# Raw w_in four pieces ahead, combine one expert earlier, last w2 in thirds of columns, every second w_out block decoded with ScalarE

## The chip, the cores and the metric

The kernel runs on one core of one Trainium2 chip. The metric is device microseconds of one execution; the time given is the median of three. One profiled execution stands beside it.

## The reference

The input goes through attention, then a soft mixture of eight experts, then a gated layer. Attention makes x, 1792 tokens of 768 columns; it is the same in both kernels and takes the first 309 us. Then:

```
# mixture: 8 experts, 4 slots each
logits = x @ phi                                # 1792 x 32
d = softmax of logits over the tokens           # dispatch
slot_input = d.T @ x                            # 32 x 768
for e in range(8):
    h = maximum(slot_input[e] @ w1[e], 0)       # 4 x 1024
    slot_out[e] = h @ w2[e]                     # 4 x 768
c = softmax of logits over the slots            # combine
y = c @ slot_out                                # 1792 x 768
# gated layer
h = y @ w_in                                    # 1792 x 2048
g = h * 1 / (1 + exp(-1.702 * h))
out = g @ w_out                                 # 1792 x 768
```

w_in and w_out arrive as 64-bit floats and are made into 32-bit ones on the chip. That is the decode spoken of below.

## The kernel before

**The expert loop** (from 309 us). For each expert e TensorE multiplies the slot inputs with w1[e] (h, L1071), VectorE makes hs = max(h, 0) scaled (L1082), TensorE transposes hs (t, L1092), VectorE copies it to hTz (L1097, L1098), and for the first six experts TensorE multiplies with w2[e] into so_ps (L1102). Fillers (L1061) keep TensorE busy in experts 5 to 7. The weights come in pieces through SP's queue (w1 L114, w2 L123) into buffers that TensorE has read last; reload (L131) asks for the next weights as soon as a half is used. The w2 of the last two experts (L117) comes in twelve pieces of 128 columns, all 1024 rows of one expert in each, and is multiplied after the loop, because slot_out is wanted there column by column.

**Decode.** w_in is cut into 24 pieces of 128 x 512, raw 512 KB each. win_load (L988) asks for one on ScalarE's queue; the tiles wst are a ring of six. win_turn is called after each of the 14 steps of an expert; from turn 29 on, every 2.2 turns, it takes one piece j: first the load of j+5, then the four steps of decode64 (L136): ScalarE scales the high words into dst (L143), VectorE shifts (L145), puts the sign in (L147) and the low bits in (L151). hs and the decode steps stand in VectorE's queue in program order.

**Combine.** combine (L1017) takes the softmax over the slots on VectorE and ScalarE at the start of expert 2, and combine_turn (L1029) makes its transposed parts, four of them, during that expert.

**After the loop** the work is put in order by a planner with a table of operations, each with an engine, a cost and a due time: last_mm (L1173) for the last w2, its copy pc (L1188), transpose pt (L1191) and sum pa (L1195), then u (L1209): slot_out @ w_in, which needs all of w_in. u0 (L1360) copies u for the first tokens. Then each token's hidden columns f come out of TensorE (L1258), ScalarE makes gg (L1266) and rounds it to gh (L1275), VectorE makes the rest gl (L1280), and TensorE multiplies with w_out (y, L1316 for the first tokens, L1299 for the rest). w_out is decoded during the first tokens, in 16 blocks of 128 rows: raw load (L1139), decode64's steps (abs on ScalarE, wd 0, 1, 2 on VectorE), whi rounds it on ScalarE (L1158) and wlo makes the rest on VectorE (L1162).

## Time and profile before

| what | us |
|---|---|
| median of 3 runs | 712.28 (710.15 to 713.52) |
| profiled execution | 712.17 |
| its span | 710.40 |
| TensorE busy | 633.2, 89% of the span |
| VectorE busy | 389.7 |
| ScalarE busy | 346.9 |

The share of busy time is a mean over stages. The table of windows gives, for a stretch, the busy time of each engine, the granted clock of TensorE as a share of full speed, the share of time that the DMA engines were busy, and the rate. A timeline row gives start, duration, engine, line, the operation with its output and inputs, and in brackets how long the engine was idle before it and what ended that.

### The profile page before, as it was taken

What the parts mean: (1) busy time and instruction counts of PE and PEld (TensorE: products, weight loads), DVE (VectorE), ACT (ScalarE), POOL (GpSimd) and SP (SyncE); (2) the same over time, 40 slices, a digit from 0 to 9 for tenths busy, and PEclk for the clock granted to TensorE, in tenths of its full rate; (3) what the DMA queues carried; (4) which work ended last, traced back from release to release, by engine and by line L of the source; (5) the groups of instructions that cost most, each with busy time, mean ns of one, the idle gap of its engine ahead of it and who ended that gap; (6) DMA issues with size and microseconds to landing.
All of it is one profiled execution on the core that took longest, in us unless ns stands there. A gap on an engine that the chain in (4) does not pass through costs nothing.

```text
span 710.4 us, 11049 instructions
## 1 busy us (share of the span) xinstructions
PE 633.2 (89%) x4091; PEld 414.3 (58%) x4091; DVE 389.7 (55%) x672; ACT 346.9 (49%) x730; POOL 193.3 (27%) x233
## 2 busy tenths in 40 slices
PE   1899999999999999986452699889999999999997
PEld 1333434443344334543221235789999999999997
DVE  5997678787887885325554712799911211211211
ACT  3766977777798764522211220766612332422432
POOL 4765988877665623200000010000000000000000
PEclk9999999999999999999666899899999999999999
DMA  9399899798989898669999982556010100100101
GB/s 225 74 178 224 195 204 232 160 199 185 228 208 192 183 253 222 240 229 398 404 403 410 330 209 90 198 172 208 22 46 1 66 2 0 67 1 1 66 2 45
DMA packets 152310, 120.30 MB, mean 169 GB/s; under 512 B 102048, under 2 KB 133024, under 8 KB 152256
## 3 DMA queue, kind: packets, MB, share of 16 engines
q1 hardware_dynamic: 148448, 106.85, 56.2%
q10 hardware_dynamic: 3744, 12.65, 4.7%
q8 instruction: 32, 0.52, 0.3%
q14 instruction: 22, 0.18, 0.1%
q0 software_dynamic: 64, 0.10, 0.1%
HBM read 92.18 MB, written 5.51 MB: 138 GB/s over the span
## 4 chain that ended last, share of the span: by engine, by line
PE 65%; DVE 14%; DMA 12%; issue 3%; ACT 3%; POOL 2%; SPq 1%; ACTq 0%; DVEq 0%; POOLq 0%
PE y L1299 26%; PE sc L517 7%; PE pv L536 6%; DMA wr<-in_moe_w_dram 6%; PE mx L498 4%; PE so_ps L1102 3%; PE pv L531 2%; PE h L1071 2%; DVE wr L502 2%; DMA wr<-wr 2%; DMA wt<-in_moe_w_dram 2%; PE y L1316 1%; DVE wr L439 1%; DVE wf L147 1%; PE f L1258 1%
## 5 line engine op out<-in xcount | busy, mean ns | idle before, releaser
L1280 DVE TENSOR_TENSOR gl<-gg,gh 128x384 fp32r<-128x384 f32 (+1 forms) x80 | 42.2, 530 | 149.0 <-ACT gh L1275 147.8
L502 DVE TENSOR_REDUCE wr<-mx 128x2 f16<-128x896 f32 x92 | 89.7, 975 | 27.8 <-PE mx L498 27.3
L1266 ACT ACTIVATE gg<-f 128x384 f32<-128x384 f32 (+1 forms) x78 | 36.5, 470 | 124.7 <-PE f L1258 121.3
L1299 PE MATMUL y<-wo,gh 128*128 128x384 f32 x352 | 75.4, 335 | 0.0
L524 POOL TENSOR_TENSOR es<-es,e 128x448 f32<-128x448 f32 x47 | 55.2, 1184 | 29.5 <-PE pv L536 10.1
L1299 PEld LDWEIGHTS y<-wo,gh 128*128 128x128 f32 x352 | 62.1, 188 | 0.0
L521 ACT ACTIVATE e<-sc,esc 128x448 f32<-128x448 f32 x96 | 56.7, 638 | 11.1 <-PE sc L517 10.3
L1299 PE MATMUL y<-wh,gl 128*128 128x384 f32 x176 | 46.8, 337 | 0.0
L1299 PE MATMUL y<-wh,gh 128*128 128x384 f32 x176 | 46.7, 336 | 0.0
L1299 PE MATMUL y<-wl,gh 128*128 128x384 f32 x176 | 46.7, 336 | 0.0
L1299 PE MATMUL y<-wo,gl 128*128 128x384 f32 x176 | 44.9, 335 | 0.0
L1275 ACT ACTIVATE gh<-gg 128x384 fp32r<-128x384 f32 (+1 forms) x78 | 39.3, 504 | 6.6 <-PE y L1299 4.2
L388 ACT ACTIVATE wr<-wr 128x512 f32<-128x512 f32 (+1 forms) x48 | 28.7, 607 | 27.1 <-DMA wr<-in_k_dram 13.5
L143 ACT ACTIVATE wi<-wst 128x512 f32<-128x512 f32 x24 | 15.7, 668 | 53.6 <-DMA wr<-in_moe_w_dram 22.4
L521 ACT ACTIVATE es<-sc,esc 128x448 f32<-128x448 f32 x54 | 33.0, 636 | 18.1 <-PE sc L517 18.1
L439 POOL TENSOR_TENSOR wr<-wr 128x512 f32<-128x512 f32 (+1 forms) x33 | 33.7, 1044 | 4.8 <-DVE wr L424 4.3
L517 PEld LDWEIGHTS <-wr 128*128 128x128 f16 (+1 forms) x224 | 18.6, 103 | 24.5 <-issue 17.4
L498 PE MATMUL mx<-wr 64*128 64x448 f16 (+1 forms) x120 | 31.0, 366 | 1.4 <-DVE wr L502 1.3
L1299 PEld LDWEIGHTS y<-wl,gh 128*128 128x128 f32 x176 | 32.0, 188 | 0.0
L1299 PEld LDWEIGHTS y<-wh,gl 128*128 128x128 f32 x176 | 32.0, 188 | 0.0
L1299 PEld LDWEIGHTS y<-wo,gl 128*128 128x128 f32 x176 | 31.8, 188 | 0.0
L1299 PEld LDWEIGHTS y<-wh,gh 128*128 128x128 f32 x176 | 31.6, 188 | 0.0
(268 smaller groups left out, 1341.1 us busy)
## 6 DMA issues: line engine op xcount, KB each, us to landing
wr<-in_moe_w_dram SPq DMA_DIRECT2D x30, 512.0 KB, 9.2
wt<-in_moe_w_dram SPq DMA_DIRECT2D x24, 512.0 KB, 8.0
wst<-in_moe_w_in_dram ACTq DMA_DIRECT2D x24, 512.0 KB, 6.8
wr<-in_moe_w_out_dram SPq DMA_DIRECT2D x15, 768.0 KB, 4.7
wr<-in_moe_w_dram SPq DMA_DIRECT2D x20, 384.0 KB, 5.5
wt<-in_moe_w_dram SPq DMA_DIRECT2D x20, 384.0 KB, 7.7
out_dram<-o SPq DMA_DIRECT2D x13, 384.0 KB, 2.3
wr<-in_q_dram SPq DMA_DIRECT2D x12, 384.0 KB, 4.8
```

The source lines that it names most:

```text
L388: nc.scalar.activation(out=sqt[p][:, 8:] if i else sqt[p][:, :8], in_=rows(p, i), func=AF.Square, scale=D ** -0.5)
L439: eng.tensor_tensor(out=n, in0=n, in1=r.to_broadcast([P, m, D]), op=ALU.mult)
L498: nc.tensor.matmul(out, q_cols(QAT[p], h, c)[:D], k_cols(KBT[p], h)[:D], start=True, stop=True)
L502: nc.vector.tensor_reduce(out=of(qb_t, p)[:, at[0]:at[-1] + 1:max(1, at[-1] - at[0]), D:D + 1], in_=MX.pop((p, g))[:, :len(at), :S], axis= ...
L517: nc.tensor.matmul(out, k_cols(a, n, c), q_cols(b, n), start=first, stop=not first)
L521: nc.scalar.activation(out=E[p, h, c], in_=SC.pop((p, h, c)), func=AF.Exp, scale=esc)
L524: on(f"e{h}{c}", p)[0].tensor_tensor(out=E[p, h, 0], in0=E[p, h, 0], in1=E[p, h, c], op=ALU.add)
L536: nc.tensor.matmul(PV[p][h * D:(h + 1) * D, :], t[:, 6 * n + 3 * h + c], E[p, h, c], start=(c == 0), stop=False)
L1266: nc.scalar.activation(out=ggt[w][:, :w[1]], in_=src[:, :w[1]], func=AF.Silu, scale=1.702)
L1275: nc.scalar.activation(out=gh[:, :w[1]], in_=ggt[w][:, :w[1]], func=AF.Copy)
L1280: nc.vector.tensor_tensor(out=G[w][1][:, :n], in0=ggt[w][:, :n], in1=G[w][0][:, :n].bitcast(F32), op=ALU.subtract)
L1299: nc.tensor.matmul(Y[t, u][:, :384], a[:, ts], b[f][:, u * 384:(u + 1) * 384], start=(f == 0 and i == 0), stop=(f == KF - 1 and i == 2),)
```

## The change

Five things are changed.

- The raw pieces of w_in: the first five loads are issued on SP's queue, where the loads during the loop stay on ScalarE's. The load at turn j is for piece j+4, no longer j+5, in the same ring of six.
- Their decode: the form called low has a second ScalarE step on the low words, in place, and two VectorE steps in place of three.
- combine is called in expert 0, after the third of its six products, and its turns in expert 1.
- The last w2 comes in thirds of 256 columns, 512 rows of one expert in a piece; the order is third, expert, half of the rows. Products of two neighbouring blocks of columns use the same pieces, and wait for both halves.
- w_out: odd blocks f use the form low. whi now follows the last decode step, and wlo follows whi. The planner's costs and due times for these are adapted.

```diff
@@ -113,10 +113,10 @@
                 r = hh * 384 + n * 128
                 nc.sync.dma_start(out=t[:, n * F1:(n + 1) * F1], in_=w1[e, r:r + 128, :])
             elif e == EL:
-                c, ee = divmod(3 * hh + n, 2)
+                c, ee, fh = (3 * hh + n) // 4, (3 * hh + n) // 2 % 2, (3 * hh + n) % 2
                 nc.sync.dma_start(
-                    out=t[:, n * F1:(n + 1) * F1].rearrange("p (f c) -> p f c", c=128),
-                    in_=w2[EL + ee, :, c * 128:(c + 1) * 128].rearrange("(f p) c -> p f c", p=128),
+                    out=t[:, n * F1:(n + 1) * F1].rearrange("p (f c) -> p f c", c=256),
+                    in_=w2[EL + ee, fh * 512:fh * 512 + 512, c * 256:(c + 1) * 256].rearrange("(f p) c -> p f c", p=128),
                 )
             else:
                 r = hh * 512 + n * 128
@@ -133,24 +133,32 @@
         if is_kept[key] is not None and nstream[0] < len(stream) - (0 if is_kept[key] else NW):
             load_all(wt[key], is_kept[key])
 
-    def decode64(dst, src, i):
+    def decode64(dst, src, low):
 
 
 
         pair = src.rearrange("p (a two) -> p a two", two=2)
         hi, lo, bits = pair[:, :, 1], pair[:, :, 0], dst.bitcast(U32)
-        if i == 0:
-            nc.scalar.activation(out=dst, in_=hi.bitcast(F32), func=AF.Copy, scale=2.0 ** -112)
-        elif i == 1:
-            nc.vector.tensor_scalar(out=bits, in0=bits, scalar1=3, scalar2=None, op0=ALU.logical_shift_left)
-        elif i == 2:
-            nc.vector.scalar_tensor_tensor(
-                out=bits, in0=hi, scalar=0x80000000, in1=bits, op0=ALU.bitwise_and, op1=ALU.bitwise_or
-            )
+        join = lambda out, a, n, b, op: nc.vector.scalar_tensor_tensor(
+            out=out, in0=a, scalar=n, in1=b, op0=op, op1=ALU.bitwise_or
+        )
+        steps = [lambda: nc.scalar.activation(out=dst, in_=hi.bitcast(F32), func=AF.Copy, scale=2.0 ** -112)]
+        if low:
+            steps += [
+                lambda: nc.scalar.activation(
+                    out=lo, in_=lo, func=AF.Copy, scale=2.0 ** -29 * (1 - 2.0 ** -16), bias=7.5 * 2.0 ** -16 - 0.5
+                ),
+                lambda: join(lo, hi, 0x80000000, lo, ALU.bitwise_and),
+                lambda: join(bits, bits, 3, lo, ALU.logical_shift_left),
+            ]
         else:
-            nc.vector.scalar_tensor_tensor(
-                out=bits, in0=lo, scalar=29, in1=bits, op0=ALU.logical_shift_right, op1=ALU.bitwise_or
-            )
+            steps += [
+                lambda: nc.vector.tensor_scalar(out=bits, in0=bits, scalar1=3, scalar2=None, op0=ALU.logical_shift_left),
+                lambda: join(bits, hi, 0x80000000, bits, ALU.bitwise_and),
+                lambda: join(bits, lo, 29, bits, ALU.logical_shift_right),
+            ]
+        return steps
 
     wi_ctx = tc.tile_pool(name="wi_p", bufs=1, reuse_waits="tile")
     wi = wi_ctx.__enter__().tile([128, KD * DFF], F32, name="wi")
@@ -985,10 +993,10 @@
         NC, NWI = 512, KD * DFF // 512
         wraw = {}
 
-        def win_load(j):
+        def win_load(j, eng):
             kc, col = divmod(j * NC, DFF)
             wraw[j] = wst.tile([128, 2 * NC], U32, tag="wst", name="wst")
-            nc.scalar.dma_start(out=wraw[j], in_=win64[kc * 128:(kc + 1) * 128, 2 * col:2 * (col + NC)])
+            eng.dma_start(out=wraw[j], in_=win64[kc * 128:(kc + 1) * 128, 2 * col:2 * (col + NC)])
 
         turns_w = [0, 0]
 
@@ -997,14 +1005,14 @@
             g, j = turns_w
             turns_w[0] += 1
             if j < NWI and g >= 29 + 2.2 * j:
-                if j + 5 < NWI:
-                    win_load(j + 5)
-                for i in range(4):
-                    decode64(wi[:, j * NC:(j + 1) * NC], wraw[j], i)
+                if 0 < j < NWI - 4:
+                    win_load(j + 4, nc.scalar)
+                for step in decode64(wi[:, j * NC:(j + 1) * NC], wraw[j], True):
+                    step()
                 turns_w[1] += 1
 
         for j in range(5):
-            win_load(j)
+            win_load(j, nc.sync)
         siT = bp.tile([128, KD, NS], F32, tag="siT", name="siT")
         for n in range(2):
             ps = ps_h.tile([128, KD // 2, NS], F32, tag="h", name="h")
@@ -1062,8 +1070,6 @@
 
         nc.scalar.activation(out=bp.tile([128, 1], F32, name="warm"), in_=rz, func=AF.Silu)
         for e in range(NE):
-            if e == 2:
-                combine()
             hps = ps_h.tile([128, Q1], F32, tag="h", name="h")
             for kk in range(KD):
                 w = wt["w1", e, kk // 3].rearrange("p (k f) -> p k f", f=F1)
@@ -1074,7 +1080,9 @@
                     )
                 if kk % 3 == 2:
                     reload("w1", e, kk // 3)
-                    if e == 2:
+                    if e == 0 and kk == 2:
+                        combine()
+                    if e == 1:
                         combine_turn(kk // 3)
                 warm_b(e, 3)
                 win_turn()
@@ -1104,7 +1112,7 @@
                         start=(e == 0 and f == 0), stop=(e == EL - 1 and f == 7),
                     )
                 if f % 4 == 3:
-                    if e == 2:
+                    if e == 1:
                         combine_turn(2 + f // 4)
                     reload("w2", e, f // 4)
                 warm_b(e, 2)
@@ -1142,7 +1150,7 @@
             if i == 0 and not h:
                 wf[f] = ring("wf", f).tile([128, DM], F32, tag="wf", name="wf")
             c = cols(f, h)
-            decode64(wf[f][:, c], wr[f][:, 2 * c.start:2 * c.stop], i)
+            decode64(wf[f][:, c], wr[f][:, 2 * c.start:2 * c.stop], f % 2)[i]()
 
         def w_hi(f, h):
             c = cols(f, h)
@@ -1150,9 +1158,9 @@
                 nc.scalar.activation(out=wh[f][:, c], in_=wf[f][:, c], func=AF.Copy)
                 return
             if f < NA:
-                if f % 2 == 0:
-                    cp["w"] = wpoolr[0].tile([128, 2, 2, DM], F32R, tag="w", name="wo")
-                wh[f], wl[f] = cp["w"][:, f % 2, 0], cp["w"][:, f % 2, 1]
+                if ("w", f // 2) not in cp:
+                    cp["w", f // 2] = wpoolr[0].tile([128, 2, 2, DM], F32R, tag="w", name="wo")
+                wh[f], wl[f] = cp["w", f // 2][:, f % 2, 0], cp["w", f // 2][:, f % 2, 1]
             else:
                 wh[f], wl[f] = (cp["wo"].tile([128, DM], F32R, name=f"w{x}{f}") for x in "hl")
             nc.scalar.activation(out=wh[f][:, c], in_=wf[f][:, c], func=AF.Copy)
@@ -1174,12 +1182,12 @@
 
             if ee == 0:
                 st["p", kk] = ps_h.tile([128, Q1], F32, tag="h", name="h")
-            i = 2 * kk + ee
-            w = wt["w2", EL, i // 3].rearrange("p (n f c) -> p n f c", n=3, c=128)
             for f in range(8):
-                g = f % 4
+                i, g = 4 * (kk // 2) + 2 * ee + f // 4, f % 4
+                w = wt["w2", EL, i // 3].rearrange("p (n f c) -> p n f c", n=3, c=256)
                 nc.tensor.matmul(
-                    st["p", kk][32 * g:32 * g + 32, :128], hTz[(EL + ee) % 2][:, f % 2, f // 2], w[:, i % 3, f],
+                    st["p", kk][32 * g:32 * g + 32, :128], hTz[(EL + ee) % 2][:, f % 2, f // 2],
+                    w[:, i % 3, g, kk % 2 * 128:kk % 2 * 128 + 128],
                     start=(ee == 0 and f < 4), stop=(ee == 1 and f >= 4),
                 )
 
@@ -1345,8 +1353,8 @@
                 i = 2 * kk + ee
                 op(("arrive", i), "SP", 1.46 if i else 0, -1, lambda: None, [("arrive", i - 1)] if i else [])
                 op(
-                    ("p", kk, ee), "PE", 0.62, kk, lambda kk=kk, ee=ee: last_mm(kk, ee), [("arrive", i)] + [("p", kk, 0)] * ee,
-                    None if ee else ("h", kk),
+                    ("p", kk, ee), "PE", 0.62, kk, lambda kk=kk, ee=ee: last_mm(kk, ee),
+                    [("arrive", kk // 2 * 4 + 2 * ee + 1)] + [("p", kk, 0)] * ee, None if ee else ("h", kk),
                 )
             op(("pc", kk), "DVE", 0.22, kk, lambda kk=kk: last_copy(kk), [("p", kk, 1)], ("hs", kk), [("h", kk)])
             op(("pt", kk), "PE", 0.14, kk, lambda kk=kk: last_turn(kk), [("pc", kk)], None, [("hs", kk)])
@@ -1380,20 +1388,22 @@
                     None if h else ("wr", f),
                 )
                 op(
-                    o("abs"), "ACT", 0.75 * n, d - 8 - first, lambda f=f, h=h: w_step(f, 0, h),
+                    o("abs"), "ACT", 0.78 * n, d - 8 - first, lambda f=f, h=h: w_step(f, 0, h),
                     [o("raw")] + ([o("abs", h=0)] if h else []) + ([("act", work[0])] if f == 1 else []),
                     None if h else ("wf", f),
                 )
                 for i in range(3):
+                    act = f % 2 and not i
                     op(
-                        o("wd", i), "DVE", (0.47, 0.87, 0.87)[i] * n, d - 6 + i - first * (i < 2), lambda f=f, i=i, h=h: w_step(f, i + 1, h),
-                        [o("wd", i - 1) if i else o("abs")] + [o("whi")] * (i == 2), None, [("wr", f)] if i == 2 else [],
+                        o("wd", i), "ACT" if act else "DVE", (0.78 if act else 0.47, 0.87, 0.87)[i] * n, d - 7 + i - first,
+                        lambda f=f, i=i, h=h: w_step(f, i + 1, h), [o("wd", i - 1) if i else o("abs")],
+                        None, [("wr", f)] if i == 2 else [],
                     )
                 op(
                     o("whi"), "ACT", 0.75 * n, d - 3 - first, lambda f=f, h=h: w_hi(f, h),
-                    [o("wd", 1)] + needs + ([o("whi", h=0)] if h else []) + ["u0"] * (f == 0),
-                )
-                op(o("wlo"), "DVE", 0.9 * n, d - 2, lambda f=f, h=h: w_lo(f, h), [o("wd", 2)], None, [("wf", f)])
+                    [o("wd", 2)] + needs + ([o("whi", h=0)] if h else []) + ["u0"] * (f == 0),
+                )
+                op(o("wlo"), "DVE", 0.9 * n, d - 2, lambda f=f, h=h: w_lo(f, h), [o("whi")], None, [("wf", f)])
         parts = lambda f, x: [(x, f) + h for h in ([()] if f else [(0,), (1,)])]
         d = 24
         for w in work:
```

On ScalarE, in the middle of the expert loop: wst are the raw tiles (a number for each piece), wi the decoded w_in. Before:

```order
432 L991 DMA wst_3738<-in_moe2_w_in_dram 128x1024
433 L143 ACTIVATE wi_79<-wst_3655 128x512
434 L991 DMA wst_3755<-in_moe2_w_in_dram 128x1024
435 L143 ACTIVATE wi_79<-wst_3673 128x512
436 L991 DMA wst_3769<-in_moe2_w_in_dram 128x1024
437 L143 ACTIVATE wi_79<-wst_3691 128x512
```

After:

```order
441 L999 DMA wst_3753<-in_moe2_w_in_dram 128x1024
442 L146 ACTIVATE wi_79<-wst_3689 128x512
443 L149 ACTIVATE wst_3689<-wst_3689 128x512
444 L999 DMA wst_3767<-in_moe2_w_in_dram 128x1024
445 L146 ACTIVATE wi_79<-wst_3704 128x512
446 L149 ACTIVATE wst_3704<-wst_3704 128x512
```

Between two loads there are now two passes of ScalarE where there was one.

On VectorE, around hs of expert 5 (hs_3899 in both). Before:

```order
459 L145 TENSOR_SCALAR wi_79<-wi_79 128x512
460 L147 SCALAR_TENSOR_TENSOR wi_79<-wst_3769,wi_79 128x512
461 L151 SCALAR_TENSOR_TENSOR wi_79<-wst_3769,wi_79 128x512
462 L145 TENSOR_SCALAR wi_79<-wi_79 128x512
463 L147 SCALAR_TENSOR_TENSOR wi_79<-wst_3791,wi_79 128x512
464 L151 SCALAR_TENSOR_TENSOR wi_79<-wst_3791,wi_79 128x512
465 L1082 TENSOR_SCALAR hs_3899<-h_3842,rz_60 128x256
466 L1097 MEMSET hTz1_3339 128x8x4
467 L1098 COPY hTz1_3339<-t_3345 128x8x4
```

After:

```order
440 L143 SCALAR_TENSOR_TENSOR wst_3789<-wst_3789 128x512
441 L143 SCALAR_TENSOR_TENSOR wi_79<-wi_79,wst_3789 128x512
442 L143 SCALAR_TENSOR_TENSOR wst_3807<-wst_3807 128x512
443 L143 SCALAR_TENSOR_TENSOR wi_79<-wi_79,wst_3807 128x512
444 L1090 TENSOR_SCALAR hs_3899<-h_3840,rz_60 128x256
445 L1105 MEMSET hTz1_3339 128x8x4
446 L1106 COPY hTz1_3339<-t_3345 128x8x4
```

hs stands behind the same pieces in both, with two steps for each in place of three; the first of them works in the raw tile.

On SP's queue, at the end of attention (wt and wr are weight buffers). Before:

```order
L123 DMA wr<-in_moe_w_dram 128x768 x6
L114 DMA wt<-in_moe_w_dram 128x1024 x6
L123 DMA wt<-in_moe_w_dram 128x768 x8
L114 DMA wt<-in_moe_w_dram 128x1024 x3
L114 DMA wr<-in_moe_w_dram 128x1024 x3
```

After:

```order
L123 DMA wr<-in_moe_w_dram 128x768 x6
L114 DMA wt<-in_moe_w_dram 128x1024 x6
L999 DMA wst<-in_moe_w_in_dram 128x1024 x5
L123 DMA wt<-in_moe_w_dram 128x768 x8
L114 DMA wt<-in_moe_w_dram 128x1024 x3
```

The five raw pieces now stand in front of the eight pieces of expert 3's w2.

On VectorE, in the output stage. Before:

```order
L1162 TENSOR_TENSOR wo<-wf,wo 128x768
L147 SCALAR_TENSOR_TENSOR wf<-wr,wf 128x768
L1280 TENSOR_TENSOR gl<-gg,gh 128x384
L145 TENSOR_SCALAR wf<-wf 128x768
L147 SCALAR_TENSOR_TENSOR wf<-wr,wf 128x768
L151 SCALAR_TENSOR_TENSOR wf<-wr,wf 128x768
```

After:

```order
L1170 TENSOR_TENSOR wo<-wf,wo 128x768
L143 SCALAR_TENSOR_TENSOR wf<-wr,wf 128x768
L1288 TENSOR_TENSOR gl<-gg,gh 128x384
L143 SCALAR_TENSOR_TENSOR wr<-wr 128x768
L1170 TENSOR_TENSOR wo<-wf,wo 128x768
L143 SCALAR_TENSOR_TENSOR wf<-wf,wr 128x768
L157 TENSOR_SCALAR wf<-wf 128x768
```

An odd block has no TENSOR_SCALAR step on VectorE any more (the two rows that name wr first and last are its steps); an even one keeps all three.

## Rows read from the trace of the kernel before

**Rows 1.** The page's first line.
```profile
span 710.4 us, 11049 instructions
```

**Rows 2.** Table of windows: stretch, its length, busy by engine, granted clock, DMA share, GB/s.
```profile
321.00:345.00 24.00, 12.40 (x148) 6.81 (x148) 14.01 (x32) 5.69 (x12) 0.00 (x0) 0.89 1.02 398
345.00:405.00 60.00, 30.19 (x292) 13.52 (x286) 31.92 (x60) 12.33 (x20) 0.00 (x0) 0.70 1.05 391
405.00:447.00 42.00, 39.46 (x487) 17.95 (x486) 11.69 (x33) 4.77 (x13) 3.45 (x17) 0.96 0.54 150
460.00:513.00 53.00, 50.01 (x276) 47.38 (x276) 50.87 (x71) 35.75 (x60) 0.00 (x0) 1.00 0.40 136
513.00:710.00 197.00, 193.43 (x1116) 193.10 (x1114) 38.76 (x75) 63.34 (x133) 0.00 (x0) 1.00 0.08 29
```

**Rows 3.** Timeline of TensorE, 358 to 428: the transposes of hs.
```profile
364.24 0.69 PE L1092 MATMUL t<-ident,hs 128*128 128x128 f32 x2 [7.13 <-DVE hTz L1097]
...
387.46 0.69 PE L1092 MATMUL t<-ident,hs 128*128 128x128 f32 x2 [13.42 <-DVE hTz L1097]
...
404.45 0.69 PE L1092 MATMUL t<-ident,hs 128*128 128x128 f32 x2 [5.25 <-DVE hTz L1097]
...
420.34 0.44 PE L1092 MATMUL t<-ident,hs 128*128 128x128 f32 x2 [0.45 <-DVE hTz L1097]
```

**Rows 4.** Timeline of VectorE, 384 to 405: hs of experts 4 and 5.
```profile
386.93 0.48 DVE L1082 TENSOR_SCALAR hs<-h,rz 128x256 f32<-128x256 f32 x1
...
403.91 0.48 DVE L1082 TENSOR_SCALAR hs<-h,rz 128x256 f32<-128x256 f32 x1
```

**Rows 5.** Timeline of ScalarE, 355 to 400: decode steps, and the load of piece 20.
```profile
367.40 0.67 ACT L143 ACTIVATE wi<-wst 128x512 f32<-128x512 f32 x1 [2.50 <-DVE wi L151]
...
370.44 0.69 ACT L143 ACTIVATE wi<-wst 128x512 f32<-128x512 f32 x1 [2.37 <-DVE wi L151]
...
384.44 0.66 ACT L143 ACTIVATE wi<-wst 128x512 f32<-128x512 f32 x1 [6.43 <-DMA wt<-in_moe_w_dram]
387.08 0.33 ACTq L991 DMA_DIRECT2D wst<-in_moe_w_in_dram  x1
```

**Rows 6.** Groups of instructions, 309 to 428: line, count, busy, mean ns, idle before.
```profile
L147 DVE SCALAR_TENSOR_TENSOR wi<-wst,wi 128x512 uint32<-128x512 uint32 x24 | 16.6, 692 | 0.8
...
L143 ACT ACTIVATE wi<-wst 128x512 f32<-128x512 f32 x24 | 15.7, 668 | 53.6 <-DMA wr<-in_moe_w_dram 22.4 <-DMA wt<-in_moe_w_dram 12.0 <-DVE wi L151 9.7
...
L145 DVE TENSOR_SCALAR wi<-wi 128x512 uint32<-128x512 uint32 x24 | 10.2, 424 | 32.0 <-ACT wi L143 32.0
...
L1043 PE MATMUL ct<-ident,cc 128*128 128x128 f32 x16 | 3.5, 360 | 13.8 <-ACT cc L1034 13.8
```

**Rows 7.** Waits of ScalarE, 340 to 400: total, times, longest.
```profile
ACT wi L143 <- DMA wr<-in_moe_w_dram: 18.5, 5, 6.6
ACT wi L143 <- DMA wt<-in_moe_w_dram: 12.0, 3, 6.4
ACT wi L143 <- DVE wi L151: 9.7, 4, 2.5
```

**Rows 8.** DMA issues of the page: count, size, median us from issue to landing.
```profile
wst<-in_moe_w_in_dram ACTq DMA_DIRECT2D x24, 512.0 KB, 6.8
```

**Rows 9.** Groups of VectorE and ScalarE, 446 to 513: w_out's decode steps.
```profile
L147 DVE SCALAR_TENSOR_TENSOR wf<-wr,wf 128x768 uint32<-128x768 uint32 x15 | 14.3, 954 | 0.2
...
L145 DVE TENSOR_SCALAR wf<-wf 128x768 uint32<-128x768 uint32 x15 | 8.3, 552 | 0.0
...
L143 ACT ACTIVATE wf<-wr 128x768 f32<-128x768 f32 x15 | 13.7, 911 | 5.9 <-DMA wr<-in_moe_w_out_dram 4.9 <-DVE wl L1162 1.0
```

**Rows 10.** Table of windows while the last w2 moves.
```profile
405.00:414.00 9.00, 8.72 (x73) 2.39 (x72) 5.35 (x10) 1.25 (x3) 3.09 (x16) 0.83 1.21 290
```

**Rows 11.** Timeline of VectorE, 475 to 490: two neighbours in the output stage.
```profile
481.91 0.55 DVE L1280 TENSOR_TENSOR gl<-gg,gh 128x384 fp32r<-128x384 f32 x1
482.38 0.55 DVE L145 TENSOR_SCALAR wf<-wf 128x768 uint32<-128x768 uint32 x1
```

## The prediction

> **What bounds the kernel now.** I read the table of windows first, then the idle times on TensorE's timeline, then what VectorE and ScalarE were doing at those moments. The profiled execution takes 712.17 us for a span of 710.40 us [rows 1], so 1.8 us lie around the span, and it stands 0.1 us under the median of 712.28; the sum below is made against 712.17.
>
> Up to 309 us both kernels issue the same work. After 513 us TensorE is busy for 193.43 of 197 us on output products that the change doesn't touch [rows 2]. What can move lies between, in two stretches.
>
> The first is the expert loop. From 321 to 405 the transfers are full (DMA share 1.02 and 1.05 at 398 and 391 GB/s), yet TensorE works only 30.19 of 60 us between 345 and 405; from 405 to 447 it works 39.46 of 42 [rows 2]. So the place to look is what TensorE waits for before 405. Its timeline shows three long idles, 7.13, 13.42 and 5.25 us, each before the transposes of hs, L1092, of experts 3, 4 and 5 [rows 3]. The row names the memset L1097 as the releaser, but that stands right behind hs on VectorE, so hs is what came late: at 386.93 and 403.91 for experts 4 and 5 [rows 4]. hs doesn't lack TensorE's result, it stands in VectorE's queue behind the decode of w_in pieces. Those start about 3.05 us apart (367.40, 370.44), and sometimes much later: 6.43 us of idle before 384.44 [rows 5]. Yet VectorE needs only 0.42 + 0.69 + 0.69 = 1.80 us a piece and ScalarE 0.67 [rows 6]. Two things stretch it. Ahead of each decode ScalarE issues the load of piece j+5 into a ring of six, which must wait for VectorE's last step on piece j-1: 9.7 us of waits on L151. And it waits for older weight transfers, 18.5 us in five waits and 12.0 in three [rows 7]: SP's and ScalarE's transfers share a few completion semaphores in program order, so a w_in load can't be issued before a weight piece has landed, and that piece was asked for only when TensorE had finished with a buffer. That is a ring: TensorE, SP, ScalarE, VectorE, TensorE. A load takes 6.8 us to land [rows 8] and is asked for five turns ahead, so the data were usually there.
>
> The second is the start of the output stage. From 460 to 513 VectorE is busy for 50.87 of 53 us and ScalarE for 35.75 [rows 2]; TensorE follows VectorE.
>
> **The change part by part.** *Loads four ahead and the shared decode.* The load at turn j is now for j+4, so its slot was freed by piece j-2: VectorE gets a turn's slack, and ScalarE can work on j while VectorE is on j-1. Per piece ScalarE has two passes, 2 x 0.67, and one issue of 0.33 [rows 5, 6], about 1.7 us; VectorE has two steps of 0.69, 1.4 us. The new steps' shapes (a pass in place on every second word) don't occur before; I price them at 0.67 and 0.69, the rows over the same words (L143 reads, L147 reads the same stride), from below by 0.42, from above by 0.95, what L147 takes for 768 elements [rows 9]. At 0.95 VectorE would need 1.9 us and hs would still keep up. So the period falls from 3.05 to about 1.7 us, less than TensorE needs. The waits on shared semaphores don't vanish, but in the changed program the transfers ahead of each load on the same semaphore were all asked for at least an expert earlier, so the ring is cut.
>
> What is late next is the transfer itself. hs of expert 5 needs piece 20. In the trace its load goes out at 387.08 [rows 5] and with 6.8 us [rows 8] lands at 393.9; by then nearly all of the weights of experts 6 and 7's first layer have come too. In the new order load 20 stands before the last two w1 pieces of expert 6 and all six of expert 7: 7 to 8 pieces of 0.524 MB, 3.7 to 4.2 MB, 9.4 to 10.7 us at 391 GB/s [rows 2], so it can land at 383 to 385. Its decode, 2 x 0.67 + 2 x 0.69 = 2.7 us, gives 386 to 388. TensorE's own pace allows that: it takes from 404.45 to 420.34, 15.9 us, from one expert's hs to the next without stalls [rows 3], and from hs of expert 3, which I put at 348 to 351.5 (its decode then waits for no load), two experts end at 380 to 388 (14 to 16 us each at a clock of 0.7 with the fillers of the later experts left out, 18 at the most). I take 387.5 for 403.91: **-16.4 us**, between -8 (half of the waits stay) and -19.
>
> The five first loads move to SP's queue, in front of expert 3's w2. It waits there anyway on TensorE's last gather at 308, as before; eight w2 pieces behind it land up to 5 x 0.524 MB, 6.6 us at 398 GB/s, later. They are wanted after hs of expert 3, 40 us on. I cost it at nothing; without that cover, up to 3 us.
>
> *Combine.* Its four long VectorE operations and ScalarE's exp now stand ahead of hs of expert 0, some 1.2 us of delay to it, while the transposes ct, which cost TensorE 13.8 us of waiting [rows 6], move from expert 2 to expert 1. There the transfers set the pace (DMA share 1.02 [rows 2]), so I count neither as gain or loss; between -2 and +2.
>
> *Last w2.* The twelve pieces now have runs of 1 KB in place of 512 bytes. Between 405 and 414 these pieces alone move at 290 GB/s while the DMA share is 1.21 [rows 10]; rows of 3 and 4 KB reach 398 [rows 2]. If a run costs a constant and a rate, 1 KB gives some 345 GB/s (an estimate from those two rows): 6.29 MB in 18.2 us in place of 21.7. The Trainium skill, DMA: Bandwidth & Descriptors, Specifications, puts the minimum for line rate at 512 bytes; by that rule the thirds would bring nothing, and the trace disagrees already at 512 bytes. With the earlier TensorE the last piece has to come earlier by as much, or it becomes the bound: I put it at 415 to 419, four microseconds before its product is wanted (the last third about 12 us into a stretch that begins at 411.4). So the term is 0 in the sum, but it is what lets the -16.4 through. In pairs the products of columns 0 and 1 wait for four pieces where they waited for one; they are in by then. From 405 to 447 TensorE is 94% busy, so the shift carries through, -0.8 for the stalls of 0.3 to 0.5 us that go: u ends at 429.6.
>
> *w_out.* For odd f ScalarE does the second step. VectorE loses 8 steps; beside each other they start 0.47 us apart ([rows 11]: gl at 481.91, L145 at 482.38) and last 0.55 [rows 9], so 3.8 to 4.4 us. VectorE is 96% busy there, so that falls to the time: **-4.0 us**. ScalarE gains 8 x 0.84 = 6.7 us (an abs pass is 0.91 with its overlap [rows 9]) on 35.75 of 53, 42.5 of 53: it has room. Rounding in whi now waits for the last step in place of the one before; VectorE has three blocks in hand. Bounds: -6 (block 0 is decoded before the first product, about 2 us of VectorE's work) to +2.7 (ScalarE in order becomes the path: 6.7 - 4.0).
>
> The Trainium skill, ScalarE: Activation LUTs, Rules for kernel authors, says to do add and mul on VectorE, not ScalarE, as VectorE is faster per element. By that rule the move would cost 6.7 where it saves 4.0, +2.7; here the rows price both near each other and VectorE is the full one, so the rule weighs little.
>
> Sum: 712.2 - 16.4 - 0.8 - 4.0 = **691 us**.
>
> **Rivals.** *Half of it.* The loads still wait on weight landings, or landing with one turn less to spare (4 x 1.7 us is 6.8, exactly a load's landing time [rows 8]) becomes what ScalarE waits for. Then the period is about 2.4 us, and hs of expert 5 comes at 396: -8 -4 = 700, with bounds 697 to 705. For it: the transfers are full, so 6.8 us may grow. Against: fewer bytes stand ahead.
>
> *The last w2 becomes the bound.* TensorE reaches the last products 17 us earlier but the pieces come at 290 GB/s as before, the last at 423 to 424 and not at 417; from there half a microsecond of products, copy, transpose, add and u step to the end of u, 5 us, and raw w_out stands behind them on the queue: ScalarE now has three passes on raw w_out, the third on the second-next block, in order before u0. u0 at 430 to 434, total 691 to 696. The rule of the Trainium skill on 512 bytes, named above, would give the same.
>
> *ScalarE is the path of the output stage.* Its 42.5 of 53 us are spread unevenly; +2.7 in place of -4: 697.
>
> *Slower.* If five w_in pieces in front of w2 of expert 3, and the slots that free later, leave the transfers idle for a while, the loss can't be recovered because they are full from 321 on: each idle microsecond costs one. With 3 us of hole, decode no quicker than before (hs of expert 5 at 404 + 3) and +2.7 in the output stage: 718. It decides from the point where hs of expert 5 comes after 408. Against it speaks that the wait of the decode is on order and not on bytes [rows 5, 7].
>
> *It doesn't do what it says:* VectorE's two steps are slower at stride 2 than the three, 2 x 0.95 against 1.80. Then the queue alone still gives the first rival's time.
>
> **How the numbers follow.** Chances: forecast 0.52 (685 to 696); half 0.18 (697 to 705); last w2 0.16 (691 to 696); ScalarE in the output stage 0.06 (694 to 699); no change, if both gains are eaten, 0.03 (709 to 715); slower 0.05 (716 to 722). The range 684 to 704 leaves out the last two, and some of the edges. A measurement of this kernel can tell 0.5%, 3.6 us, from no change: faster 0.92, same 0.03, slower 0.05.
>
> **What would show it.** Right: decode starts about 1.7 to 2 us apart in the expert loop; no idle over 3 us before the transposes of hs for experts 3 to 5; hs of expert 5 near 387.5; u0 near 430; first output product near 433; VectorE's busy time 57 to 58 us over the blocks of w_out. Wrong: idles of 5 us or more before hs with ScalarE waiting for wst to land (half), a wait of the last products on w2 pieces (last w2), TensorE waiting for ScalarE's whi in the output stage (ScalarE), DMA share under 0.9 between 321 and 345 (slower).

## The result: 20 us less, three quarters of it in the expert loop

The changed kernel takes 691.25 us (689.73 to 693.83, four runs) against 711.21 for the kernel before: a ratio of 0.972, interval 0.9673 to 0.9766. The forecast was 691. Its profiled execution, 693.83 us with a span of 692.1, is the slowest of the four.

Attention doesn't end at the same time in every execution (309.2 to 312.8 us after the start in the traces here). So below, dates in the loop are also counted from the end of the last slot-input product (L1013 before, L1021 after; start plus duration of its row on TensorE's timeline): 310.7 in the trace before, 312.8 after. So counted, hs of expert 5 comes at 78.5 us where it came at 93.2, u0 at 121.1 for 136.3: -14.7 and -15.2. From the first output product to the end of the span it takes 255.2 us for 260.4: -5.2. The -15.2 at u0 and this -5.2, together -20.4, are the gain, and the medians agree with it (-20.0). First the windows of the changed kernel, stage by stage as in [rows 2]; the columns are the stretch, its length, busy time of PE, PEld, DVE, ACT, POOL, granted clock, DMA share and GB/s.

```profile
321.00:345.00 24.00, 20.98 (x293) 11.49 (x284) 11.40 (x24) 9.95 (x20) 0.00 (x0) 1.00 0.90 348
345.00:389.00 44.00, 21.25 (x211) 9.61 (x211) 19.39 (x33) 16.79 (x28) 0.00 (x0) 0.69 1.03 406
389.00:430.00 41.00, 37.02 (x455) 16.41 (x451) 12.98 (x34) 9.42 (x20) 3.44 (x17) 0.96 0.92 327
...
440.00:493.00 53.00, 52.59 (x298) 51.92 (x297) 49.99 (x69) 45.03 (x73) 0.00 (x0) 1.00 0.45 157
493.00:692.00 199.00, 195.10 (x1126) 194.78 (x1124) 39.20 (x75) 64.17 (x135) 0.00 (x0) 1.00 0.08 29
```

In the output stage (440 to 493) TensorE works 52.59 of 53 us, where it worked 50.01 [rows 2]: it no longer follows VectorE. (These 53 us begin 3.1 us behind the first output product, those of [rows 2] 10.0 us behind it. Taken 10 us behind it here too, from 447 to 500, TensorE works 53.00 and ScalarE 41.91.) But the expert loop isn't what was forecast. TensorE still idles half of 345 to 389, and there is a stretch with a DMA share of 0.90, where it was 1.02. TensorE's timeline, the transposes of hs of experts 3 to 6, shows the idles that answer to [rows 3]:

```profile
355.57 0.69 PE L1100 MATMUL t<-ident,hs 128*128 128x128 f32 x2 [12.30 <-DVE hTz L1105]
...
377.04 0.69 PE L1100 MATMUL t<-ident,hs 128*128 128x128 f32 x2 [11.61 <-DVE hTz L1105]
...
391.86 0.44 PE L1100 MATMUL t<-ident,hs 128*128 128x128 f32 x2 [2.16 <-DVE hTz L1105]
...
407.86 0.44 PE L1100 MATMUL t<-ident,hs 128*128 128x128 f32 x2 [0.45 <-DVE hTz L1105]
```

12.30 and 11.61 us are left where 7.13 and 13.42 stood; the third idle fell from 5.25 to 2.16, and TensorE reaches expert 3 sooner. That is most of the loop's gain: counted from the slot inputs, hs of expert 3 comes 10.8 us earlier (42.2 for 53.0), hs of expert 5 14.7. The decode of a piece starts 2.86 us after the one before it, in the mean from the first piece to piece 20 (331.4 to 388.5 us); before it was 3.73 (324.4 to 399.0). ScalarE's timeline tells why the decode wasn't even-paced: the load of a piece goes out behind a wait for a weight transfer, and the decode stands behind it.

```profile
350.72 0.34 ACTq L999 DMA_DIRECT2D wst<-in_moe_w_in_dram  x1
351.10 0.66 ACT L146 ACTIVATE wi<-wst 128x512 f32<-128x512 f32 x1 [5.56 <-DMA wr<-in_moe_w_dram]
351.66 0.64 ACT L149 ACTIVATE wst<-wst 128x512 uint32<-128x512 uint32 x1
```

The new steps cost what they were priced at (groups of instructions, 309 to 430: count, busy, mean ns, idle before):

```profile
L143 DVE SCALAR_TENSOR_TENSOR wst<-wst 128x512 uint32<-128x512 uint32 x24 | 16.6, 691 | 28.8 <-ACT wst L149 26.3 <-DMA wt<-in_moe_w_dram 2.1 <-DMA wr<-in_moe_w_dram 0.4
L146 ACT ACTIVATE wi<-wst 128x512 f32<-128x512 f32 x24 | 16.2, 675 | 36.4 <-DMA wr<-in_moe_w_dram 15.7 <-DMA wt<-in_moe_w_dram 6.6 <-DMA wst<-in_moe_w_in_dram 5.8
...
L149 ACT ACTIVATE wst<-wst 128x512 uint32<-128x512 uint32 x24 | 15.9, 661 | 0.0
```

### The profile page after: what moved, and what is told of

Its sections match the earlier page's. It is cut to its first block, busy times and chain, and to the rows that moved or that the text cites. A ratio compares the mean times of both kernels' runs of the same rounds, so it can differ in the third digit from the quotient of the medians.

```text
span 692.1 us, 11043 instructions
## 1 busy us (share of the span) xinstructions
PE 630.0 (91%) x4089; PEld 414.5 (60%) x4089; DVE 377.5 (55%) x640; ACT 365.8 (53%) x762; POOL 191.9 (28%) x233
## 4 chain that ended last, share of the span: by engine, by line
PE 74%; DMA 12%; DVE 9%; ACT 2%; issue 1%; SPq 1%; POOL 0%; ACTq 0%; DVEq 0%; POOLq 0%
PE y L1307 27%; PE y L1324 7%; PE sc L525 7%; PE pv L544 7%; PE mx L506 4%; DMA wr<-in_moe_w_dram 4%; PE pv L539 3%; DMA wr<-wr 3%; PE so_ps L1110 2%; PE h L1077 2%; DVE wr L510 2%; PE f L1266 2%; DMA wt<-in_moe_w_dram 2%; PE ms L591 2%; PE ms L590 1%; DVE wr L447 1%
## 5 line engine op out<-in xcount | busy, mean ns | idle before, releaser
L1288 DVE TENSOR_TENSOR gl<-gg,gh 128x384 fp32r<-128x384 f32 (+1 forms) x80 | 42.2, 530 | 149.1 <-ACT gh L1283 148.3
L529 ACT ACTIVATE es<-sc,esc 128x448 f32<-128x448 f32 x54 | 32.9, 634 | 18.3 <-PE sc L525 18.1
L143 DVE SCALAR_TENSOR_TENSOR wst<-wst 128x512 uint32<-128x512 uint32 x24 | 16.6, 691 | 28.8 <-ACT wst L149 26.3
```

The costliest lines, as they stand in the source:

```text
L529: nc.scalar.activation(out=E[p, h, c], in_=SC.pop((p, h, c)), func=AF.Exp, scale=esc)
L1288: nc.vector.tensor_tensor(out=G[w][1][:, :n], in0=ggt[w][:, :n], in1=G[w][0][:, :n].bitcast(F32), op=ALU.subtract)
```

## The experiments

All dates in the table are starts in us from each run's own profile, counted from the end of the slot-input products (e3 and e5 are experts 3 and 5); "first y to end" is the time from the first output product to the end of the span; "weight waits" is the time that ScalarE waited for weight transfers ahead of a w_in decode, 325 to 400 us. Each ratio is to runs of the kernel before that were taken beside it; their medians lie between 711.1 and 712.2.

Two things limit how finely the table can be read. u2 has the very loop of the change, and its hs of expert 5 comes at 77.3 for 78.5. In the profile of the change TensorE's granted clock was 0.50 from 309 to 313 us, which is its 1.2 GHz level, and 0.54 to 318 (1.00 in u2); it fell after 307, with TensorE busy for 0.52 of the two microseconds before, and hs of expert 0 comes at 5.2 us there, at 4.1 in u2. And the intervals of u1, u2, u4, u6 and x1 overlap that of the change. Run by run, all of u2 and p1 lie above the four runs of the change and all of u4, v2 and v4 below them; u1, u6 and x1 lie above but for one run each, and u3 and v3 lie among them.

| run | median us | ratio to before (interval) | hs of e3 | hs of e5 | last w2 lands | u0 | first y to end | weight waits |
|---|---|---|---|---|---|---|---|---|
| before | 711.2 | 1 | 53.0 | 93.2 | 109.7 | 136.3 | 260.4 | 34.4 |
| the change | 691.25 | 0.972 (0.967 to 0.977) | 42.2 | 78.5 | 107.7 | 121.1 | 255.2 | 22.3 |
| u1_w2_columns128 | 695.82 | 0.976 (0.971 to 0.980) | 42.5 | 78.5 | 111.6 | 122.0 | 256.2 | 21.4 |
| u2_wout_old | 696.13 | 0.976 (0.972 to 0.981) | 41.3 | 77.3 | 107.5 | 120.9 | 258.5 | 22.9 |
| u3_combine_back | 690.87 | 0.971 (0.968 to 0.974) | 43.9 | 79.4 | 105.0 | 122.2 | 255.1 | 18.3 |
| u4_three_steps | 687.81 | 0.964 (0.959 to 0.968) | 39.7 | 74.3 | 108.5 | 118.9 | 255.0 | 10.7 |
| u5_old_queue | 712.93 | 1.002 (1.000 to 1.005) | 59.5 | 99.5 | 111.7 | 142.0 | 255.0 | 31.2 |
| u6_first_on_act | 694.89 | 0.976 (0.974 to 0.979) | 48.4 | 82.5 | 111.8 | 125.1 | 255.1 | 19.7 |
| v2_three_six | 685.85 | 0.963 (0.960 to 0.966) | 38.5 | 73.0 | 109.1 | 118.7 | 255.1 | 7.8 |
| v3_three_combine_back | 690.45 | 0.971 (0.968 to 0.974) | 42.0 | 78.4 | 105.2 | 121.7 | 254.9 | 25.7 |
| x1_spare_pass | 695.59 | 0.977 (0.974 to 0.980) | 42.3 | 80.2 | 106.7 | 123.6 | 254.9 | 21.1 |
| p1_queue_alone | 698.42 | 0.981 (0.977 to 0.984) | 41.9 | 78.2 | 109.5 | 122.1 | 258.4 | 23.5 |
| d1_w2_thirds_alone | 711.78 | 1.000 (0.998 to 1.001) | 52.2 | 92.4 | 105.4 | 136.5 | 258.0 | 32.2 |
| v4_three_six_again | 685.52 | 0.963 (0.960 to 0.967) | 37.2 | 72.9 | 108.7 | 117.5 | 255.4 | 11.9 |

**The queue.** First the loads alone taken back:

```diff
-                if 0 < j < NWI - 4:
-                    win_load(j + 4, nc.scalar)
+                if j + 5 < NWI:
+                    win_load(j + 5, nc.scalar)
...
-            win_load(j, nc.sync)
+            win_load(j, nc.scalar)
```

> The changed kernel with the loads of w_in as before: the five first ones on ScalarE's queue, then at turn j the one for j+5; the shared decode stays. Theory A: the slot of piece j+5 again waits for VectorE's last step on j-1 and the load for older weight pieces, so the loop falls back most of the way, hs of expert 5 at 398 to 403, time 698 to 703. Rival C, the shared decode is what counts: hs of expert 5 at 391 to 394, time 691 to 694.

712.93 us: the whole gain is gone, though the output stage keeps its 255.0. Theory A (the order of the loads) holds against C (the shared decode), and the fall is larger than it said. The reverse, the new order of loads alone on the kernel before:

> The kernel before with one part of the change alone: the first five loads on SP's queue and the load at turn j for j+4. Decode, combine, last w2 and w_out as before. Theory A (order of the loads is the gain of the expert loop): hs of expert 5 comes 12 to 16 us earlier against the start of the loop, the last w2 at 290 GB/s takes back some 3 us at its end, the output stage stays at 260 us: time 698 to 702. Rival: alone it gives under half of that, 705 to 709.

698.42 us, 13.8 below the 712.19 of its neighbours, with hs of expert 5 at 78.2: as early as in the whole change. (Its profiled execution, 694.98 us, is the fastest of its four, so its dates flatter it.) So the expert loop's gain is the queue's. p1 leaves combine in expert 2, and TensorE still waits 9.1 us there for ct (13.8 before [rows 6], nothing in the change), yet hs of expert 3 comes at 41.9: these waits don't set the pace. Only the five first loads taken back to ScalarE:

> The changed kernel with the five first w_in loads on ScalarE's queue again. Theory A, only the order among the transfers from 336 us on counts: the five pieces land a few us later or earlier, 10 us and more before their decode at 331, time 690 to 692.5. Rival F, the five loads on SP ahead of expert 3's weights are part of the gain: time 694 to 700.

694.89 us is in the range of rival F, and the reason isn't when the pieces land. u6 and u5 differ only in the loads during the loop, for j+4 or for j+5: 694.89 for 712.93, hs of expert 5 at 82.5 for 99.5. So of the 21.7 us by which u5 is slower than the change, 18.0 hang on asking one piece further ahead, and 3.6 on the place of the five first loads. For these 3.6 ScalarE's timeline shows the five loads ahead of combine's exp:

```profile
307.54 4.48 ACTq L999 DMA_DIRECT2D wst<-in_moe_w_in_dram  x5
312.06 1.28 ACT L1071 ACT_TABLE_LOAD   x1 [5.53 <-PE h L1077]
...
314.87 0.63 ACT L1030 ACTIVATE lg<-lg 128x512 f32<-128x512 f32 x1
```

The five issues hold ScalarE for 4.48 us (four have gone out by 309.3, the fifth goes out at 311.69), and two loads of function tables (ACT_TABLE_LOAD, 1.28 us each) follow. The exp comes at 314.87, VectorE needs it for the rest of combine, and hs of expert 0 stands behind that. TensorE waits 5.52 us:

```profile
317.89 0.69 PE L1100 MATMUL t<-ident,hs 128*128 128x128 f32 x2 [5.52 <-DVE hs L1090]
```

In the change ScalarE is done with the table loads before VectorE has the exp's input, and TensorE's wait is 0.64:

```profile
314.46 0.63 ACT L1030 ACTIVATE lg<-lg 128x512 f32<-128x512 f32 x1 [1.31 <-DVE lg L1029]
```

```profile
318.54 0.44 PE L1100 MATMUL t<-ident,hs 128*128 128x128 f32 x2 [0.64 <-DVE hs L1090]
```

Counted from the slot inputs, the exp comes at 5.2 us in u6 and at 1.6 in the change, 3.6 apart as the medians are. So combine in expert 0 and loads on SP belong together, and u5 lost both, which is part of why it lost more than p1 gained.

**The shared decode.** Loads as changed, w_in's decode in three VectorE steps:

```diff
-                for step in decode64(wi[:, j * NC:(j + 1) * NC], wraw[j], True):
+                for step in decode64(wi[:, j * NC:(j + 1) * NC], wraw[j], False):
```

> The changed kernel with w_in decoded in the old form, one ScalarE pass and three VectorE steps (1.80 us of VectorE a piece), loads and all else as changed. Theory A, order and rate of the transfers set the pace of the expert loop: a piece lands every 2 to 3 us, VectorE keeps up, hs of expert 5 within 1 us of 391.3, time 690.5 to 693. Rival C, the shared decode is what made hs earlier: hs of expert 5 at 396 or later, time 696 to 702.

687.81 us fits neither theory: it is faster than the whole change. (The two intervals overlap, from 0.9673 to 0.9684; those of v2 and v4, which decode this way too, don't overlap the change's.) hs of expert 5 comes 4.2 us earlier, though VectorE works 1.80 us a piece in place of 1.38. ScalarE's waits, 325 to 400 us, first of the kernel before, then of the change, then of this run (total, times, longest):

```profile
ACT wi L143 <- DMA wr<-in_moe_w_dram: 22.4, 6, 6.6
ACT wi L143 <- DMA wt<-in_moe_w_dram: 12.0, 3, 6.4
```

```profile
ACT wi L146 <- DMA wr<-in_moe_w_dram: 15.7, 5, 5.6
...
ACT wi L146 <- DMA wt<-in_moe_w_dram: 6.6, 3, 2.3
```

```profile
ACT wi L146 <- DMA wst<-in_moe_w_in_dram: 14.9, 7, 3.0
...
ACT wi L146 <- DMA wr<-in_moe_w_dram: 7.8, 1, 7.8
...
ACT wi L146 <- DMA wt<-in_moe_w_dram: 2.9, 1, 2.9
```

34.4, 22.3 and 10.7 us, where hs of expert 5 comes at 93.2, 78.5 and 74.3. In this run ScalarE waits mostly for its own earlier loads, wst (14.9 us). The weight waits alone don't order the runs, though: v3 has 25.7 us of them with hs of expert 5 at 78.4, u3 18.3 with 79.4. To see whether it is ScalarE's second pass or the form of VectorE's steps, the pass was put back without its use, over the high words, with the three steps kept:

```diff
...
+                steps = decode64(wi[:, j * NC:(j + 1) * NC], wraw[j], False)
+                hi = wraw[j].rearrange("p (a two) -> p a two", two=2)[:, :, 1].bitcast(F32)
+                steps.insert(1, lambda: nc.scalar.activation(out=hi, in_=hi, func=AF.Copy))
...
```

> The run u4_three_steps (687.8 us) with one ScalarE pass more for each piece of w_in, a copy of the raw high words onto themselves between the first pass and the VectorE steps; VectorE's three steps stay. Theory G, what the shared decode cost is ScalarE's second pass: it pushes each next load of w_in back in ScalarE's queue and in the order in which the transfers share their semaphores. Then the time goes back to 690.5 to 694 and ScalarE waits for weight transfers for 15 us or more in the loop. Rival H, ScalarE has room and the cost lies in the form of the two VectorE steps: 687 to 689.

695.59 us, weight waits 21.1, hs of expert 5 at 80.2: that is theory G, 1.6 us beyond its range. The pass is the cost. Whether by ScalarE's time or by the place that it gives to the loads among the other transfers stays open: no run here moves the loads' place alone.

**Combine.** Back in expert 2, with the shared decode and with three steps:

> The changed kernel with combine and its turns back in expert 2. Theory D, TensorE is the limit from 309 to 331 us (it is 92% busy and more there, and the DMA share falls to 0.78 and 0.66 between 326 and 336 because all buffers are full): without combine's transposes in expert 1 TensorE frees buffers earlier, the hole in the transfers shrinks by 2 to 3 us, but expert 2 has the stalls before ct again, which cost nothing while transfers set the pace: time 688 to 690. Rival E, the stalls in expert 2 delay the decode and hs of expert 3 as before: time 694 to 699.

> The run u4_three_steps with combine and its turns back in expert 2. Theory D (TensorE the limit from 309 to 331, the hole in the transfers shorter): 684.5 to 686.5. Rival E (the stalls before ct in expert 2 delay decode and hs): 690 to 696.

With the shared decode it makes no difference (690.87), with three steps it costs 2.6 us (690.45 for 687.81, in rival E's range; the intervals overlap from 0.9677 to 0.9684 only). Theory D is half right. The hole in the transfers, a stretch in which their share falls, is there in the change, and gone in u3 (windows 326 to 336, the change first, then u3):

```profile
326.00:331.00 5.00, 4.62 (x55) 2.41 (x50) 1.47 (x6) 0.88 (x4) 0.00 (x0) 1.00 0.78 309
331.00:336.00 5.00, 4.67 (x73) 2.38 (x66) 3.08 (x6) 4.21 (x9) 0.00 (x0) 1.00 0.66 220
```

```profile
326.00:331.00 5.00, 2.73 (x34) 1.46 (x33) 3.41 (x10) 2.74 (x7) 0.00 (x0) 1.00 1.03 413
331.00:336.00 5.00, 4.48 (x34) 2.12 (x32) 3.31 (x7) 2.98 (x7) 0.00 (x0) 0.66 1.04 407
```

How deep the hole is differs between executions. u2, with the loop of the change and TensorE's clock at 1.00, has little of it:

```profile
326.00:331.00 5.00, 5.00 (x64) 2.71 (x62) 1.22 (x4) 2.85 (x8) 0.00 (x0) 1.00 0.96 341
331.00:336.00 5.00, 4.08 (x68) 2.13 (x63) 4.09 (x9) 3.15 (x6) 0.00 (x0) 1.00 0.98 370
```

With combine in expert 2 the last w2 lands 2.7 us earlier (105.0 for 107.7). The depth of the hole doesn't make that, as u2's lands at 107.5; what does stays open. But u0 doesn't come earlier, since TensorE is later than the transfers then (17.2 us from that landing to u0, for 13.3). Theory D took the transfers for the limit; with the shared decode they aren't.

**The sixth load first**, on top of the three steps:

> The changed kernel with w_in decoded in three VectorE steps (the run u4_three_steps, 687.8 us) and with six loads issued first in place of five, so that the load of piece 5 stands on SP's queue at 311 and not on ScalarE's at 329. If the transfers set the pace and the hole at 326 to 331 us is one of full buffers, 0.524 MB at 400 GB/s, 1.3 us, are moved ahead of it: time 686 to 687. Rival: the hole only gets longer by as much or another wait comes: 687.5 to 689.

> The kernel of the run v2_three_six once more (685.9 us in 4 runs, 684.8 to 689.4), to narrow it against the changed kernel (691.25) and against u4_three_steps (687.8). If the sixth load is worth its 1.3 us: 685.5 to 687. If not: 687.5 to 688.5.

685.85 and 685.52, ratios 0.9632 and 0.9634 with intervals from 0.960 to 0.967; u4's was 0.9639. A gain from the sixth load can't be told from nothing. But this kernel is faster than the change (0.9603 to 0.9665 against 0.9673 to 0.9766), by nearly 6 us, and is the best one here.

**The last w2.** Thirds taken back, and thirds alone on the kernel before:

```diff
-                c, ee, fh = (3 * hh + n) // 4, (3 * hh + n) // 2 % 2, (3 * hh + n) % 2
+                c, ee = divmod(3 * hh + n, 2)
...
```

> The changed kernel with one part undone: the last w2 again in twelve pieces of 128 columns (runs of 512 bytes). Theory A, the transfers set the pace from 336 us to the end of the last w2: twelve pieces of 0.524 MB at 290 GB/s in place of 355 take 21.7 in place of 17.7 us, the last one lands 4 us later, at 424 to 425, and u0 comes at 437 to 438 in place of 433.9: time 694 to 696. Rival B, after the loop TensorE's own order of products sets the pace and the pieces are hidden: u0 stays within 1 us, time 690.5 to 692.5.

> The kernel before with the thirds of columns of the last w2 alone. In the kernel before the last piece lands at 420.4 and its products start at 429, TensorE being late: the pieces come some 3 us earlier and nothing waits for them, time 710 to 712. Rival: what bounds is the queue as a whole, and earlier w2 pieces let w_out's blocks and the last products start earlier: 706 to 709.

Alone they give nothing, 711.78 for 712.19, though the last piece lands 4.3 us earlier (105.4 for 109.7): 31.1 us then pass until u0. In the change, taking them back costs 4.6 us by the medians, with overlapping intervals, and 2.7 in the profiles: 0.9 at u0, 0.8 from there to the first output product (3.85 us for 3.05, ScalarE now has a pass on a raw block, 0.89 us, ahead of a table load), and 1.0 in the output stage. The size is open between these; the sign in the profile is theory A's. There the last landing binds: u0 follows it by 10.4 us, as in u4. The rate, while these pieces move, of the change and then of u1:

```profile
404.00:413.00 9.00, 8.55 (x94) 3.37 (x92) 1.08 (x4) 0.00 (x0) 0.00 (x0) 1.00 1.08 347
413.00:421.00 8.00, 7.19 (x110) 4.37 (x108) 1.40 (x6) 0.00 (x0) 0.00 (x0) 1.00 1.08 365
```

```profile
401.00:413.00 12.00, 11.02 (x115) 4.82 (x114) 1.79 (x7) 0.00 (x0) 0.00 (x0) 1.00 1.15 288
413.00:421.00 8.00, 8.00 (x148) 5.05 (x149) 1.44 (x6) 0.00 (x0) 0.00 (x0) 1.00 1.18 301
```

**w_out decoded as before:**

```diff
-            decode64(wf[f][:, c], wr[f][:, 2 * c.start:2 * c.stop], f % 2)[i]()
+            decode64(wf[f][:, c], wr[f][:, 2 * c.start:2 * c.stop], False)[i]()
...
```

with the order of whi and wlo and the planner's numbers of before.

> The changed kernel with w_out decoded as before: three VectorE steps for every block, whi after the second of them, wlo after the third, the planner's costs and due times as before. If VectorE is what the output stage waits for, TensorE's idle before whi and wlo comes back and the stage from the first y to the end takes 260 us in place of 255: time 695 to 697. Rival: ScalarE's longer queue gives back what VectorE saves, and the stage got shorter by its start alone: time 690.5 to 692.5.

The time is 696.13 us, and the output stage takes 258.5 us for 255.2. TensorE's idles before whi and wlo are back, six of them, the first and the last:

```profile
452.47 1.31 PE L1324 MATMUL y<-wo,gh 128*128 128x384 f32 x6 [0.47 <-ACT wo L1166]
...
492.09 1.32 PE L1324 MATMUL y<-wl,gh 128*128 128x384 f32 x6 [0.28 <-DVE wl L1170]
```

In the change one is left, 0.41 us at 443.13. So ScalarE had the room: over the same stretch behind the first output product as in [rows 2] it is busy for 41.91 of 53 us, 6.2 more than before, where 6.7 more were forecast.

## Why the prediction was right, and where its steps were not

**What bounds the kernel**: this was right. hs stands behind the decode, the loads behind weight transfers, and TensorE behind VectorE in the output stage; taking the loads back (u5) and the w_out decode back (u2) brings each one back.

**hs of expert 5, -16.4**: it measured -14.7 from the start of the loop. But the way there was not the one described. The step that failed is "the ring is cut" and the period of 1.7 us. The period measured 2.86 us, and of the signs of being right two failed: the decode starts aren't 1.7 to 2 us apart, and two idles of 12 us are left before the transposes of hs. ScalarE still waits 22.3 us for weights, in eight waits. I reasoned from the order that the transfers ahead on the same semaphores are asked for long before; yet asked for isn't landed. The load at 350.72 shown above goes out 0.1 us after a weight piece on its semaphore has landed, and that piece had been asked for 9.0 us earlier, at 341.63. While the transfers are full (1.03 at 406 GB/s) an SP load waits for a w_in load on its semaphore as well as the other way round (waits of SP's queue, 325 to 410 us):

```profile
SPq L123 <- DMA wst<-in_moe_w_in_dram: 6.5, 3, 4.4
```

My first rival (half of it) named this wait. What kept the sum near is the other argument, that of bytes ahead of piece 20. Its load goes out with eight weight pieces asked for behind it:

```profile
380.11 0.33 ACTq L999 DMA_DIRECT2D wst<-in_moe_w_in_dram  x1
```

It lands 6.8 us later, at 386.9, which is 384.7 by the dates of the trace before, where 383 to 385 was forecast. From there to hs of expert 5 it takes 4.4 us in place of 2.7, and that is the 1.7 us that are missing. Piece 19 is decoded just ahead of it, so that its own first pass starts at 388.51:

```profile
387.37 0.68 ACT L146 ACTIVATE wi<-wst 128x512 f32<-128x512 f32 x1 [1.98 <-DMA wst<-in_moe_w_in_dram]
...
388.51 0.68 ACT L146 ACTIVATE wi<-wst 128x512 f32<-128x512 f32 x1
```

**Shared decode**: counted as part of the gain; it is a loss of 3.4 us (687.81 for 691.25). The error is to have priced ScalarE's second pass by its length, 0.67 us in a period of 1.7, where ScalarE also issues the loads in the same order. In the output stage, where it issues none, the same pass pays. The Trainium skill, ScalarE: Activation LUTs, Rules for kernel authors, would keep an add or a product on VectorE. Its reason, time per element, for which it gives a factor in bf16, isn't what decided: over 128 x 512 of these 32-bit words the passes take 0.66 us on ScalarE and 0.69 on VectorE.

**Five first loads, "nothing"**: this was mis-sized. No run shows a cost of their new place, but the old place would have held up combine's exp, now that it stands in expert 0: 3.6 us.

**Combine, -2 to +2**: it came within its bounds, 0 in the change (691.25 for 690.87 in u3); it earns 2.6 only with the three steps.

**Last w2**: the rate was right, 347 to 365 GB/s for an estimate of 345, and so was that it earns nothing by itself and lets the rest through. Its last landing was put at 415 to 419; it came at 420.6 in its own trace, which is 418.4 by the dates of the trace before: inside, at the late end. The hole that the rival "slower" feared did come, with a share of 0.78 and 0.66 between 326 and 336, but the last landing doesn't follow its depth (u2). The term of 0 held since u0 was TensorE's to set: it follows the last landing by 13.3 us, where 10.4 are enough in u1 and u4.

**u0, -17.2** (the -16.4 and the -0.8): it measured -15.2 from the start of the loop.

**w_out, -4.0**: it measured -5.2 for the stage, of which undoing it returns 3.3; the other 2 us are in every run with an earlier last w2 or earlier TensorE (258.0 in d1, 258.4 in p1, both with the old decode). ScalarE's wait for raw w_out, 4.9 us in the trace before [rows 9], isn't what they are: u2, p1 and d1 still have 3.9 to 4.3 us of it. What they have no more is one long idle of TensorE ahead of whi in the trace before:

```profile
476.51 1.33 PE L1316 MATMUL y<-wo,gh 128*128 128x384 f32 x6 [1.63 <-ACT wo L1158]
```

The longest such idle in u2, p1 and d1 is 0.48 us. Why it went stays open.

So the total fell on the forecast in part by luck, because two errors had opposite signs: 2 us too much in the loop, 1 too little in the output stage. Within the loop, one part that was counted as gain is a loss, and the sum came near only because it had been bounded by when piece 20 lands.

## What to carry to other kernels

An engine that issues transfers can have less room than its busy share says. Here each pass put on ScalarE stood ahead of the next load (a spare pass, 687.81 to 695.59 us), and as the transfers of two queues share completion semaphores, one late load held the other queue too. Before moving work to an idle engine, look at what it issues. And the parts of one change are not a sum: thirds of w2 were worth nothing alone, the place of combine depended on where the first loads were issued, and the queue carried both.

## What the runs showed of the hardware

Transfers into SBUF in pieces of 0.524 MB moved at 288 to 301 GB/s with runs of 512 bytes (u1), at 347 to 365 with 1 KB (the change), and at 391 to 413 in stretches of pieces with rows of 3 and 4 KB ([rows 2] and u3), each at a DMA share above 1. The Trainium skill, DMA: Bandwidth & Descriptors, Specifications, gives 512 bytes as enough for line rate; the measurement differs: the step from 512 bytes to 1 KB gave a fifth more. ScalarE's pass in place over every second 32-bit word took 0.661 us for 128 x 512, as much as one that reads strided and writes in a row (0.675).
